# Linear attention and SwiGLU on one core: which engine makes the third part of a hidden chunk

## The chip, the cores and the metric

The kernel runs on one core of a Trainium2 chip. The metric is the device time of one execution in microseconds (us). The core has TensorE (PE, matrix products into PSUM), VectorE (DVE), ScalarE (ACT), GpSimd (POOL) and SyncE (SP); SP, POOL and ACT also issue DMA transfers, each from a queue of its own that works in order. A row `PEld` is the loading of weights into TensorE, which runs beside its products.

## The reference

```python
# attention: q, k, v are (4, 4, 1088, 32); S1, S2 are (8, 32)
def phi(x):
    a = np.einsum('rd,bhsd->bhsr', S1, x)
    b = np.einsum('rd,bhsd->bhsr', S2, x)
    return np.einsum('bhsi,bhsj->bhsij', a, b).reshape(*x.shape[:-1], 64)
q_p, k_p = (phi(q), phi(k))
kv = np.einsum('bhsf,bhsd->bhfd', k_p, v)
z = np.sum(k_p, axis=2)
num = np.einsum('bhsf,bhfd->bhsd', q_p, kv)
den = np.einsum('bhsf,bhf->bhs', q_p, z)[..., None] + 1e-06
x = (num / den).transpose(0, 2, 1, 3).reshape(4352, 128)
# feed-forward: w_gate, w_val are (128, 1536); w_out is (1536, 128)
g = x @ w_gate
silu = g * (1.0 / (1.0 + np.exp(-g)))
out = silu * (x @ w_val) @ w_out
```

All of it is float32.

## The kernel before

The tokens are cut into ten blocks: 0 to 2 are the first batch (384, 320 and 384 tokens), 3 to 8 have 480 tokens each and 9 (`LAST`) has 384. The inner dimension of 1536 is cut into 12 chunks of 128. A *unit* is one block with one chunk j: the gate and value products, a SiLU on ScalarE, and the hidden chunk h = silu * value on VectorE. Later a *down* product multiplies h by its piece of `w_out` and adds it to the block's sum in PSUM. The first 90 us or so hold the attention of the first batch and the units of blocks 0 to 2; the attention of the other batches is strewn between later units.

**The loop this is about** runs over 84 units, y = 0 to 83, twelve for each of blocks 3 to 9 (`line`); block 6 is y = 36 to 47 (from about 172 us), block 7 is 48 to 59, block 8 is 60 to 71 and block 9 is 72 to 83 (from about 248 us). In each pass the program text issues, in this order: the first two matmuls of unit y+1 with ScalarE's scaling of their PSUM pair (`start_unit`, L983 and L986); then `finish_unit` of unit y, which begins with the work on the list `before[y]`, goes on with four matmuls (L995, L996), the SiLU (L998) and VectorE's product (L1003), frees the PSUM pair, and ends with the work on the list `behind[y]`; then up to two stores from the list `going`; then the down products that keep some six chunks waiting (`todo`). Three PSUM pairs serve the units in turn, so the matmuls of unit y+3 can start when L1003 of unit y has read its pair. Every engine works through its own instructions in this order.

**Products in parts.** A matmul of full float32 shows as two records of about 0.4 us each at 480 columns. A chunk on the list `DOWN` goes by three cheaper matmuls instead, on rounded parts. `cut_hidden(y, i, j)` makes the parts of h: the high part h1 is -CUT/BETA times h, rounded; h0 = BETA * h1 + h is what is left; hd = h1 + h0. `down` then multiplies hd (L1063), h1 (L1065) and h0 (L1066) with parts of the weights. The first goes to one bank of PSUM and the other two to another bank, which `copy_out` (ScalarE, L1088) moves to SBUF and `put_together` (VectorE, L1098) adds, after which `store` transposes the sum (L1124) and sends it out (L1134).

- h1 of a chunk of unit y is made in unit y+1: on VectorE, last on the list `before` (L953), for even j outside block 5; on ScalarE, on the list `behind` (L955), for the others.
- hd, for every block but the last: SP copies h1 to hd's place by DMA in unit y+1 (L957); in unit y+2 VectorE makes h0 (L960), and POOL issues a DMA that adds h0 to what lies there (L966). In the last block a VectorE addition makes hd (L964).
- `DOWN` holds seven chunks of block 5, chunks 1 to 10 of blocks 6, 7 and 8, and chunks 1 to 7 of the last block (its first 256 columns; the rest goes through `straight` at the end).

Parts of h live in eight sets of buffers used in turn. Two steps a block prepare the next block's tokens (`cut_tokens`: L865 on ScalarE, L868 on POOL, L873 on VectorE). A finished block gives four stores, or eight where it crosses from one batch into the next.

Of the kernel before, what the change touches and what calls it, by code (L numbers as in the profile page):

```python
# [13 lines left out]
ALU = mybir.AluOpType  # L14
# [5 lines left out]
def kernel(  # L20
# [28 lines left out]
    nc = tc.nc  # L49
# [24 lines left out]
    LAST = len(blocks) - 1  # L74
# [110 lines left out]
    def load_next():  # L185
# [36 lines left out]
        out=ident[:], in_=ident[:], pattern=[[-1, P]], base=0, channel_multiplier=1,  # L222
# [594 lines left out]
    def whole(ap):  # L817
        return ap.bitcast(FP32)
# [67 lines left out]
    line = list(range(HEAD, len(blocks)))  # L886
    FINE = range(1, NCH - 1)
    DOWN = [(line[2], j) for j in (2, 4, 5, 6, 8, 9, 10)]
    DOWN += [(i, j) for i in line[3:6] for j in FINE]
    DOWN += [(LAST, j) for j in range(1, 8)]  # L890
    down_parts = {}
    h_parts = {}
    h_sets = []
    before, behind = {}, {}

    def add_to(where, y, f):
        where.setdefault(y, []).append(f)
# [38 lines left out]
    def cut_hidden(y, i, j):  # L936

        if not h_sets:
            x = []
            for tag in ("kld", "qld", "vld", "kT", "qT"):  # L940
                t = const.tile([P, 2, WB], F32R, tag=tag, name="h" + tag, bufs=1)
                x += [t[:, k, :] for k in range(2)]
            for tag, n in (("late", 8), ("wg", 3), ("wv", 3)):
                t = const.tile([P, n, WB], F32R, tag=tag, name="h" + tag, bufs=1)
                x += [t[:, k, :] for k in range(n)]
            h_sets.extend(x[k : k + 3] for k in range(0, len(x), 3))
        n = SPLIT if i == LAST else blocks[i][1]
        h_sets.append(h_sets.pop(0))
        h1, h0, hd = h_parts[i, j] = [x[:, 0:n] for x in h_sets[-1]]
        h = hidden[i, j][:, 0:n]  # L950
        small = -CUT / BETA
        if j % 2 == 0 and i != line[2]:
            add_to(before, y + 1, lambda: nc.vector.tensor_scalar(h1, h, small, None, op0=ALU.mult))  # L953
        else:
            add_to(behind, y + 1, lambda: nc.scalar.activation(h1, h, AF.Copy, scale=small))  # L955
        if i != LAST:
            add_to(behind, y + 1, lambda: nc.sync.dma_start(out=whole(hd), in_=whole(h1)))  # L957

        def rest():
            nc.vector.scalar_tensor_tensor(  # L960
                out=h0, in0=whole(h1), scalar=BETA, in1=h, op0=ALU.mult, op1=ALU.add
            )
            if i == LAST:
                nc.vector.tensor_tensor(out=hd, in0=whole(h1), in1=whole(h0), op=ALU.add)  # L964
            else:
                nc.gpsimd.dma_start(out=hd, in_=h0, accum_op=ALU.add)  # L966

        add_to(before, y + 2, rest)


# [6 lines left out]
    def start_unit(i, j):  # L977

        n = blocks[i][1]
        xd = x_parts[i][2][:, 0:n]  # L980
        ps = sums_of[i, j] = pair((i, j))[:, :, 0:n]
        for k, w in enumerate((wg, wv)):
            nc.tensor.matmul(  # L983
                ps[:, k], w_parts[id(w), j // 3][2][:, j % 3, :], xd, start=True, stop=True
            )
        nc.scalar.activation(ps, ps, AF.Copy, scale=-1.0 / WHOLE)  # L986

    def finish_unit(i, j, y=None):
        n = blocks[i][1]
        x1, x0, _ = (x[:, 0:n] for x in x_parts[i])  # L990
        ps = sums_of.pop((i, j))
        now(before, y)
        for k, w in enumerate((wg, wv)):
            w1, wb = (w_parts[id(w), j // 3][t][:, j % 3, :] for t in range(2))
            nc.tensor.matmul(ps[:, k], w1, x1, start=False, stop=False, skip_group_check=True)  # L995
            nc.tensor.matmul(ps[:, k], wb, x0, start=False, stop=True, skip_group_check=True)  # L996
        sg = fpool.tile([P, WB], FP32, tag="sg", name="sg", bufs=5)[:, 0:n]
        nc.scalar.activation(sg, ps[:, 0], AF.Silu, scale=WHOLE)  # L998
        slot_of[i, j] = slots.pop(0)
        hj = slot_of[i, j]  # L1000
        hidden[i, j] = hj
        todo.append((i, j))
        nc.vector.scalar_tensor_tensor(  # L1003
            out=hj[:, 0:n], in0=ps[:, 1], scalar=WHOLE, in1=sg, op0=ALU.mult, op1=ALU.mult
        )
        let_go((i, j))
        now(behind, y)
        if (i, j) in DOWN:
            cut_hidden(y, i, j)
# [38 lines left out]
    def down(y=None):  # L1048

        i, j = todo.pop(0)  # L1050
        n = SPLIT if i == LAST else blocks[i][1]
        first = i not in acc
        if first:
            acc[i] = bank("g2" if i == 1 or i in line[2::2] else "acc")
        made[i] = made.get(i, 0) + 1
        mine = [c for c in range(NCH) if (i, c) in DOWN]
        if mine and j == mine[0]:
            acc[i, "p"] = bank("acc" if i in line[2::2] else "g2")
        sides = dict(start=first, stop=(made[i] == NCH))
        if j in mine:  # L1060
            w1, wb, wd = [down_parts[x][:, FINE.index(j), :] for x in ("w1", "wb", "wd")]
            h1, h0, hd = h_parts.pop((i, j))
            nc.tensor.matmul(acc[i][:, 0:n], wd, hd, **sides)  # L1063
            p = acc[i, "p"][:, 0:n]
            nc.tensor.matmul(p, w1, h1, start=(j == mine[0]), stop=False)  # L1065
            nc.tensor.matmul(p, wb, h0, start=False, stop=(j == mine[-1]))  # L1066
            if j == mine[-1]:
                copy_out(y, i, n)
        else:
            nc.tensor.matmul(acc[i][:, 0:n], wo[:, j, :], hidden[i, j][:, 0:n], **sides)  # L1070
        if i != LAST:
            hidden.pop((i, j))
            slots.append(slot_of[i, j])
        if made[i] == NCH:
            if mine:
                put_together(y, i, n)
            elif i == HEAD - 1:

                add_to(behind, 1, lambda: store(i, n))
            else:  # L1080
                store(i, n)
# [36 lines left out]
    going = []  # L1118
# [42 lines left out]
    for h in range(H):  # L1161
# [13 lines left out]
        out=s12[:],  # L1175
# [73 lines left out]
    def parts_of(n):  # L1249

        for _ in range(n):
            if ahead[0] not in ("pe", "end"):
                ahead[0] = next(att, "end")

    def group():
        while ahead[0] != "pe":
            ahead[0] = next(att)
        ahead[0] = next(att, "end")
# [143 lines left out]
    for y in range(END):  # L1402
        if y in GROUPS:
            group()
        at = [(line[x // NCH], x % NCH) for x in (y, y + 1) if x < END]
        if y in WIDE:
            finish_unit(*at[0], y)
        if y + 1 < END:
            start_unit(*at[1])
        if y not in WIDE:  # L1410
            finish_unit(*at[0], y)
        for send in going[:2]:
            send()
        del going[:2]
        for _ in range(2):

            if len(todo) > min(6 + (todo[0] == (line[1], 0)), END - y + 1):
                down(y)
        parts_of(y < EASY or y % 2 == 0)
        for gen in token_steps.get(y, ()):  # L1420
            next(gen, None)
        if y in range(20, 30):
            next(down_steps, None)
# [43 lines left out]
```

## Time and profile before

| | |
|---|---|
| three runs | 280.11, 279.72, 280.16 us; median 280.11 |
| profiled execution | 280.31 us, of which the span from first to last instruction is 278.6 |
| PE busy | 269.8 us (97% of the span), 2195 instructions |
| DVE busy | 203.0 us (73%), 388 |
| ACT busy | 192.4 us (69%), 342 |
| POOL busy | 91.0 us (33%), 114 |
| DMA | 32.51 MB; 28.9% of 16 engines' span on SP's and ACT's queue, 19.0% on POOL's |
| transfers of parts | each 240 KB; 37 copies issued by SP (medians by buffer 2.3 to 4.2 us from issue to landing) and 37 accumulations by POOL (3.2 to 4.5) |

Every row of a timeline has start, length, engine, line, operation, what is written and read, shapes, and in brackets the idle time just before with what ended it. Lengths of neighbouring matmuls, and of neighbouring VectorE operations, overlap, so the distance between starts is what one of them costs. Buffers appear under the names of the tiles whose space they reuse (`hlate`, `hwv`, `hqld` and so on are all parts of h).

### The profile page before, as it was taken

To read this page: it belongs to the slowest core of one execution; us is meant where nothing else is said; L and a number is where in the kernel's file an instruction comes from. 1 tells how busy PE (TensorE), PEld (TensorE's weight loads), DVE (VectorE), ACT (ScalarE), POOL (GpSimd) and SP (SyncE) were. 2 spreads that over 40 slices of the span, in tenths; PEclk is the share of its full clock that TensorE was granted. 3 is DMA by queue.
4 is the path that set the end of the run, shared out by engine and by line. 5 is a ranking of instruction groups with operands and counts; after the bars stand their busy time and mean duration, and the time that the engine had idled before them with its cause. 6 is when DMAs were issued, how large, how long until landed. Compare 5 with 4: busy or idle time off the path is not lost.

```text
span 278.6 us, 5961 instructions
## 1 busy us (share of the span) xinstructions
PE 269.8 (97%) x2195; PEld 200.6 (72%) x2195; DVE 203.0 (73%) x388; ACT 192.4 (69%) x342; POOL 91.0 (33%) x114
## 2 busy tenths in 40 slices
PE   8899999999999999999999999999999999998994
PEld 7645566667885787777677678768877878886894
DVE  3997988899798764897637688559668758873771
ACT  3468566463684877677489889778779869875870
POOL 3314322169150720530055231342343343423000
PEclk9999999999999999999999999999999999999999
DMA  6583195222240043000200169867988997998121
GB/s 193 165 229 93 39 275 176 82 80 87 36 100 11 1 119 90 1 0 3 35 17 1 38 167 186 176 161 179 225 183 206 217 213 174 217 226 181 22 37 28
DMA packets 36797, 32.51 MB, mean 117 GB/s; under 512 B 21024, under 2 KB 34848, under 8 KB 36768
## 3 DMA queue, kind: packets, MB, share of 16 engines
q1 hardware_dynamic: 30784, 22.93, 28.9%
q0 software_dynamic: 5328, 9.10, 19.0%
q8 instruction: 17, 0.28, 0.4%
q10 hardware_dynamic: 656, 0.10, 0.2%
q14 instruction: 12, 0.10, 0.1%
HBM read 11.41 MB, written 2.23 MB: 49 GB/s over the span
## 4 chain that ended last, share of the span: by engine, by line
PE 82%; DMA 10%; DVE 4%; ACT 2%; issue 1%; SPq 0%; POOLq 0%
PE PS L1070 19%; PE PS L983 12%; PE PS L995 12%; PE PS L1019 12%; PE PS L996 11%; DMA hwv<-hwv 5%; DMA hlate<-hlate 2%; PE PS L1063 2%; PE PS L1065 2%; PE PS L1066 2%; PE PS L354 2%; PE PS L342 2%; PE PS L776 2%; PE PS L388 2%; DMA kld<-in_k_dram 2%
## 5 line engine op out<-in xcount | busy, mean ns | idle before, releaser
L986 ACT ACTIVATE PS<-PS 128x960 f32<-128x960 f32 (+1 forms) x90 | 83.2, 925 | 35.0 <-PE PS L983 34.2
L1003 DVE SCALAR_TENSOR_TENSOR hbuf<-PS,sg 128x480 f32<-128x480 f32 (+1 forms) x87 | 55.5, 638 | 51.0 <-ACT sg L998 49.4
L1070 PE MATMUL PS<-hbuf,wo 128*128 128x480 f32 (+3 forms) x126 | 52.6, 514 | 0.0
L998 ACT ACTIVATE sg<-PS 128x480 f32<-128x480 f32 (+1 forms) x90 | 49.6, 551 | 1.6 <-PE PS L996 1.3
L983 PE MATMUL PS<-xd,graw 128*128 128x480 f32 (+1 forms) x69 | 37.1, 537 | 0.0
L983 PE MATMUL PS<-xd,wd 128*128 128x480 f32 (+1 forms) x90 | 33.5, 372 | 0.0
L996 PE MATMUL PS<-x,wb 128*128 128x480 f32 (+1 forms) x90 | 33.5, 372 | 0.0
L995 PE MATMUL PS<-x,w 128*128 128x480 f32 (+1 forms) x90 | 33.4, 371 | 0.0
L1070 PEld LDWEIGHTS PS<-hbuf,wo 128*128 128x128 f32 x126 | 23.6, 189 | 6.1 <-issue 0.4
L996 PE MATMUL PS<-x,graw 128*128 128x480 f32 (+1 forms) x69 | 25.5, 370 | 0.0
L1019 PE MATMUL PS<-xT,wg 128*128 128x384 f32 (+1 forms) x60 | 23.5, 473 | 0.1
L983 PEld LDWEIGHTS PS<-xd,wd 128*128 128x128 f32 x90 | 17.0, 189 | 9.1 <-issue 5.1
L1019 PE MATMUL PS<-xT,wv 128*128 128x384 f32 (+1 forms) x60 | 23.1, 468 | 0.3 <-DVE wv L286 0.3
L1023 ACT ACTIVATE sg<-PS 128x384 f32<-128x384 f32 (+1 forms) x24 | 11.2, 467 | 13.2 <-PE PS L1019 12.4
L966 POOL DMA_DIRECT2D hlate<-hlate x14 | 12.2, 895 | 24.0 <-DMA hlate<-hlate 6.9
L995 PEld LDWEIGHTS PS<-x,w 128*128 128x128 f32 x90 | 16.9, 187 | 2.2
L996 PEld LDWEIGHTS PS<-x,wb 128*128 128x128 f32 x90 | 16.9, 188 | 2.1
L983 PEld LDWEIGHTS PS<-xd,graw 128*128 128x128 f32 x69 | 13.0, 188 | 7.5 <-ACT PS L986 4.3
L995 PE MATMUL PS<-x,graw 128*128 128x480 f32 (+1 forms) x48 | 18.0, 376 | 0.0
L1019 PEld LDWEIGHTS PS<-xT,wv 128*128 128x128 f32 x60 | 11.2, 190 | 7.3 <-DVE hbuf L1034 0.8
L1019 PEld LDWEIGHTS PS<-xT,wg 128*128 128x128 f32 x60 | 10.9, 190 | 7.7 <-issue 1.1
L995 PE MATMUL PS<-x,gphq 128*128 128x480 f32 (+1 forms) x42 | 16.0, 381 | 0.1
(224 smaller groups left out, 525.3 us busy)
## 6 DMA issues: line engine op xcount, KB each, us to landing
hlate<-hlate POOLq DMA_DIRECT2D x14, 240.0 KB, 3.6
kld<-in_k_dram SPq DMA_DIRECT2D x4, 544.0 KB, 4.3
hlate<-hlate SPq DMA_DIRECT2D x9, 240.0 KB, 3.1
vld<-in_v_dram SPq DMA_DIRECT2D x12, 144.0 KB, 4.8
qld<-in_q_dram SPq DMA_DIRECT2D x3, 544.0 KB, 4.8
raw<-in_moe_w_out_dram SPq DMA_DIRECT2D x4, 384.0 KB, 4.7
hqld<-hkld SPq DMA_DIRECT2D x5, 240.0 KB, 4.2
hqld<-hkld POOLq DMA_DIRECT2D x5, 240.0 KB, 3.5
```

The lines of the kernel that those rows point to most:

```text
L342: nc.tensor.matmul(ps[32 * a : 32 * a + 32, 96 * (c - c0) : 96 * (c - c0) + 96], qT[:, 4 * c + a, :], s123[:, a : a + H, :, :].rearrange(" ...
L354: nc.tensor.matmul(ps[32 * a : 32 * a + 64, 64 * (c - c0) : 64 * (c - c0) + 64], kT[:, c, a : a + 2, :].rearrange("p a t -> p (a t)"), s12 ...
L966: nc.gpsimd.dma_start(out=hd, in_=h0, accum_op=ALU.add)
L983: nc.tensor.matmul(ps[:, k], w_parts[id(w), j // 3][2][:, j % 3, :], xd, start=True, stop=True)
L986: nc.scalar.activation(ps, ps, AF.Copy, scale=-1.0 / WHOLE)
L995: nc.tensor.matmul(ps[:, k], w1, x1, start=False, stop=False, skip_group_check=True)
L996: nc.tensor.matmul(ps[:, k], wb, x0, start=False, stop=True, skip_group_check=True)
L998: nc.scalar.activation(sg, ps[:, 0], AF.Silu, scale=WHOLE)
L1003: nc.vector.scalar_tensor_tensor(out=hj[:, 0:n], in0=ps[:, 1], scalar=WHOLE, in1=sg, op0=ALU.mult, op1=ALU.mult)
L1019: nc.tensor.matmul(o[:, 0:n], w[:, j, :], xT[:, t0 : t0 + n], start=True, stop=True)
L1023: nc.scalar.activation(sg[:, 0:n], g[:, 0:n], AF.Silu)
L1070: nc.tensor.matmul(acc[i][:, 0:n], wo[:, j, :], hidden[i, j][:, 0:n], **sides)
```

## The change

For blocks 6, 7 and 8 the DMA way of making hd stays for odd j alone. For even j VectorE makes hd by an addition (L964 of the kernel before) right after h0, and neither SP nor POOL issues a transfer. Block 5 keeps DMA for all its seven chunks, the last block keeps VectorE for all. Where h1 is made on VectorE it is put at the head of the list `before` instead of its end. The last block's chunk 8 joins `DOWN`. Of the waiting stores one is sent in each unit instead of two.

```diff
-    DOWN += [(LAST, j) for j in range(1, 8)]
+    DOWN += [(LAST, j) for j in range(1, 9)]
...
         small = -CUT / BETA
-        if j % 2 == 0 and i != line[2]:
-            add_to(before, y + 1, lambda: nc.vector.tensor_scalar(h1, h, small, None, op0=ALU.mult))
-        else:
+        carried = i == line[2] or i != LAST and j % 2
+        if carried or j % 2:
             add_to(behind, y + 1, lambda: nc.scalar.activation(h1, h, AF.Copy, scale=small))
-        if i != LAST:
+        if carried:
             add_to(behind, y + 1, lambda: nc.sync.dma_start(out=whole(hd), in_=whole(h1)))
+        if not carried and j % 2 == 0:
+            high = lambda: nc.vector.tensor_scalar(h1, h, small, None, op0=ALU.mult)
+            before.setdefault(y + 1, []).insert(0, high)
 
         def rest():
             nc.vector.scalar_tensor_tensor(
                 out=h0, in0=whole(h1), scalar=BETA, in1=h, op0=ALU.mult, op1=ALU.add
             )
-            if i == LAST:
+            if carried:
+                nc.gpsimd.dma_start(out=hd, in_=h0, accum_op=ALU.add)
+            else:
                 nc.vector.tensor_tensor(out=hd, in0=whole(h1), in1=whole(h0), op=ALU.add)
-            else:
-                nc.gpsimd.dma_start(out=hd, in_=h0, accum_op=ALU.add)
...
-        for send in going[:2]:
-            send()
-        del going[:2]
+        if going:
+            going.pop(0)()
```

## The prediction

> **What bounds the kernel now.** I read the busy strip of the page first, then the chain of waits, then the timeline of each engine at the places where the chain leaves TensorE.
>
> ```profile
> PE   8899999999999999999999999999999999998994
> DVE  3997988899798764897637688559668758873771
> ACT  3468566463684877677489889778779869875870
> PEclk9999999999999999999999999999999999999999
> DMA  6583195222240043000200169867988997998121
> ```
>
> TensorE (PE) is filled from end to end at full clock; no other engine is. The DMA engines are idle until slice 23 (about 160 us) and then 80 to 90% busy up to 258 us: that is the stretch in which hidden chunks go through DMA to become hd. So removed matmul time or removed PE waits are worth their length; work on other engines costs only where PE comes to wait for it.
>
> The chain in order of time shows where PE does wait (start, length, what):
>
> ```profile
> 197.93 0.51 ACT PS L986
> 198.44 3.86 DMA hwv<-hwv
> 202.36 0.49 issue
> 202.85 4.38 DMA hwv<-hwv
> 207.28 0.48 PE PS L1063
> ...
> 246.12 3.55 DMA hqld<-hkld
> 249.71 0.48 PE PS L1063
> ...
> 251.49 3.65 DMA hlate<-hlate
> 255.69 3.23 DMA hlate<-hlate
> 258.97 0.48 PE PS L1063
> ```
>
> One part's two transfers in a row, a copy on SP's queue (L957) and an accumulating one on POOL's (L966), end after PE wants the matmul with hd (L1063). The PE timeline gives the size, for instance here:
>
> ```profile
> 253.65 0.34 PE L996 MATMUL PS<-x,wb 128*128 128x384 f32 x1
> 254.61 0.49 PE L1063 MATMUL PS<-hqT,dparts 128*128 128x480 f32 x1 [0.62 <-DMA hqT<-hkT]
> 254.94 0.38 PE L1065 MATMUL PS<-hkT,dparts 128*128 128x480 f32 x1
> ```
>
> Matmuls overlap, so the measure is start to start: 0.175 us after a 384-column one and 0.217 after 480. Here it is 0.96 and then 0.33, so 0.785 + 0.11 = 0.89 lost. Counted so, all stalls before an L1063 are 0.94 (at 206.22), 0.06 (209.34), 0.58 (227.11), 0.35 (249.28), 0.59 (251.35), 0.89 (253.65), 0.61 (256.24) and 0.33 (258.56): **4.35 us**. The down matmul of unit y-6 stands at the end of unit y, so these are chunks 9 and 10 of block 6 (units 51, 52), chunk 7 of block 7 (unit 61), and chunks 6 to 10 of block 8 (units 72 to 76). A check on the last five: L983 starts at 248.40 and 259.72, 11.32 us for five units; a unit with nothing late is 6 x 0.173 + 3 x 0.217 = 1.69, five are 8.45, so 2.87 lost against 2.77 listed.
>
> **The change, part by part.**
>
> (1) Even chunks of blocks 6, 7, 8 (numbered from 0) lose both transfers: 15 copies and 15 accumulations of 240 KB. Even stalls go with them: 0.06 + 0.35 + 0.89 + 0.33 = 1.63 us.
>
> (2) Odd chunks keep both transfers but lose their neighbours. The need: the down matmul is wanted at 206.43 for block 6's chunk 9, whose copy is issued at 198.44, so 8.0 us. Quiet transfers of this size in the table of DMA issues take 2.3 (hlate<-hqT) and 3.2 (hvld<-hvld); the pause between them was 0.5. That is 6.0 us, 2.0 early. With the table's medians for crowded ones (3.1 and 3.6) it is 7.2, still 0.8 early. The tail is tighter: units there last 1.69 instead of 1.95. SP's timeline shows why block 8 suffers most: two stores (L1134, 1.5 to 1.9 us a pair) stand ahead of each copy, and chunk 9's copy left at 249.31 though ACT had made its h1 by 247.11.
>
> With one store per unit, at most some 0.95 stands ahead, so it leaves near 247.6; 6.0 later is 253.6, 7.2 later 254.8. It is wanted at 256.42 less the 1.83 of earlier stalls gone, 254.6. So 1.0 early or 0.2 late. The odd stalls, 0.94 + 0.58 + 0.59 + 0.61 = 2.72, go to between 0 and 0.2; from the other side, if load did not matter at all, they would stay at 2.72. I take 0, by the quiet rows, since half the traffic goes.
>
> The Trainium skill ("DMA: Bandwidth & Descriptors", section on the anatomy of one DMA) has a fixed 2.0 us plus bytes over 436 GB/s, 2.6 us for 240 KB, mostly fixed: taken alone it says that less load buys little. The trace's same-sized transfers range from 2.2 to 5.3 us, so here load is what counts; the page's 2.6 + 0.5 + 2.6 would also be in time.
>
> (3) VectorE gains 15 subtractions hd (L964) of 480 columns. The trace has L964 at 256 columns only, 0.425 us; the 480-column add with one operand in PSUM (L1098) is 0.65:
>
> ```profile
> 190.04 0.65 DVE L873 SCALAR_TENSOR_TENSOR xd<-x,xT 128x480 fp32r<-128x480 f32 x1
> 190.61 0.65 DVE L960 SCALAR_TENSOR_TENSOR hlate<-hqT,hbuf 128x480 fp32r<-128x480 f32 x1
> 191.18 0.67 DVE L1124 STREAM_TRANSPOSE o<-sum 128x480 f32<-128x480 f32 x1
> 191.77 0.37 DVE L953 TENSOR_SCALAR hlate<-hbuf 128x480 fp32r<-128x480 f32 x1
> 192.06 0.65 DVE L1003 SCALAR_TENSOR_TENSOR hbuf<-PS,sg 128x480 f32<-128x480 f32 x1
> ```
>
> Back to back they start 0.57 apart (0.29 to 0.33 for L953). So hd costs 0.57, 8.6 us in all, at most 0.65, 9.8 us. Two units last 2 x 1.95 = 3.90; VectorE works 2 x (0.58 + 0.57) + 0.33 = 2.63 of them now and 3.20 after, 82%. What it must not do is finish L1003 late: in unit y it frees the PSUM pair that the first matmuls of unit y+3 need, with 1.1 to 1.2 us of slack in a plain unit (197.44 + 0.66 against the L983 at 199.24). I added 0.57 to each unit from 42 to 72 that has an even rest, against the SiLU that L1003 waits for. Plain units absorb it. The worst is unit 43 (the rows above): already full, after unit 42 that gained hd and an L1098; L1003 would start 0.75 us after its SiLU, with 0.4 us of slack left. With 0.65 for each operation and no overlap, units 43 to 46 and 67 to 72 run out of slack and PE loses about 0.8. So 0 to 0.8; I take 0.1, near the overlapped starts.
>
> (4) The even high part moves to the head of its unit. It follows the L1003 that makes its input on the same engine, so it waits for nothing. Behind it stand the rest of the unit before, an odd chunk's accumulation on POOL, and L1003; each moves 0.33 later, against the 2.0 and 0.8 us of (2). In units 51 and 63 its old place met POOL's subtraction:
>
> ```profile
> 206.30 1.44 POOL L868 TENSOR_TENSOR x<-xT,x 128x480 fp32r<-128x480 f32 x1
> 206.40 1.61 DVE L953 TENSOR_SCALAR hkT<-hbuf 128x480 fp32r<-128x480 f32 x1
> ```
>
> 1.61 (1.22 in unit 63) instead of 0.40; at the head it would start near 205.9 and be through. That spares VectorE up to 1.2 + 0.8 us, or nothing if POOL, with fewer transfers to issue, starts sooner. Both units have slack, so 0 on PE either way.
>
> The skill speaks against more VectorE work here ("SBUF — State Buffer", section on the two separate sides): an operation with two SBUF inputs, as hd is, and a GpSimd one that reads SBUF exclude each other for their whole length. L960, also with two SBUF inputs, ran 205.84 to 206.49 across that POOL start unstretched. By the rule one POOL subtraction a block could hold hd for 1.44, up to 0.4 past the slack each time, 1.2 us more; by the row nothing.
>
> (5) Stores one per unit: the same number of issues on SP, worked into (2). Block 8's four go in units 79 to 82, long before the last stores at 275.35. 0, hidden by the tail of matmuls; without that cover an SP issue of 0.5.
>
> (6) Chunk 8 of the last block: the fp32 pair of 256 columns (2 x 0.215 = 0.43) becomes three of 0.117 (0.35): 0.08 less. VectorE gets 0.25 + 0.42 + 0.42 more in units 81 and 82, where it idled 1.19 before the L1003 at 269.74. Were that cover gone, the late thing would be this chunk's L1063, by those 1.1 at most. The sum's copy (L1088) moves one unit later, behind the last SiLU; it is needed only at 273.24. 0.
>
> **Sum.** 4.35 + 0.08 - 0.1 = 4.3 off the profiled execution, 280.31 us (span 278.6 and 1.7 around it): 276.0. It stood 0.2 above the median of 280.11, so 275.8. Bounds: 280.11 - 4.43 = 275.7 at best, with 0.4 for noise 275.3; at worst within this case 275.8 + 0.2 + 0.7 = 276.7.
>
> **Rivals.**
>
> Odd transfers stay late. For it: they are still issued in the same units, and a quiet pair needs 6.0 of about 7 us in the tail. Against it: the 2.0 us to spare at unit 51. All 2.72 staying gives 275.8 + 2.7 = 278.5; half of it 277.2.
>
> VectorE becomes the bound, and the kernel is slower. Place: blocks 6 to 8, the pairs of units. It decides once 3.20 exceeds 3.90, so when hd takes over 1.27 us. Price: if each hd were stretched as L953 was beside POOL (1.2 more, 1.77), a pair takes 4.40, 15 x 0.50 = 7.5 us lost, less 4.4 gained: 283.2. For it: that one row, and unit 43 being full already. Against it: L960 keeps 0.65 in all its groups, and POOL gets fewer issues.
>
> No change that shows: under 0.2%, 0.56 us, is all a measurement here can tell. The waits go, but hd at about 1.55 us loses what they gave: 15 x 0.28 = 4.2; 280.
>
> **How the numbers follow.** Forecast 0.64, odd transfers late 0.20, no change 0.05, VectorE bound 0.11. Faster 0.84, same 0.05, slower 0.11. Range 275.3 to 278.6: the forecast's own (275.3 to 276.7) and the second case up to all odd stalls staying; what is left out is 0.16.
>
> **What would show it.** Right: no L1063 that waits for a DMA from 200 to 260 us; copies near 2.3 and accumulations near 3.2 us; DMA digits of 4 to 6 there; L964 of 480 columns near 0.65 with starts 0.57 apart; L1003 after its SiLU within 0.1 us in most units and 0.8 in unit 43; L953 never above 0.5. Wrong: an L983 of units 45 to 48 waiting for L1003; L1063 of odd chunks still late; L964 above 1.2.

## The result and the profile after

Four runs gave 276.66 us (276.21 to 277.50) against 280.13 (279.72 to 280.78) before: a ratio of 0.988, 95% interval 0.985 to 0.991. On another chip, beside other experiments, the changed kernel gave 276.74 against 280.56, 0.987 (0.985 to 0.988). The profiled execution took 276.21 us with a span of 274.5, so 4.1 less than the profiled one before.

The strip of the page, in the same 40 slices:

```profile
PE   6999999999999999999999999999999999999994
DVE  3997988989788774887655677668958986996981
DMA  6673196121231043000110048853464472565021
```

The DMA digits from 199 to 254 us (slices 29 to 36, counted from 0) fell from 7 to 9 down to 2 to 7, VectorE's rose to 9 in places, PE's have no dip left. The chain of waits followed from 196 to 262 us, by line, holds nothing but matmuls; before, 23 us of that stretch (35% of 66) were DMA:

```profile
by line: PE PS L998 22.0%; PE PS L997 21.9%; PE PS L985 21.5%; PE PS L1065 9.5%; PE PS L1068 9.4%; PE PS L1067 9.4%; PE PS L1072 6.8%
```

(The new lines: the matmul with hd is L1065, the unit's first matmuls L985, the SiLU L1000, its product L1005, the high part L958, h0 L962, hd L968, the copy L956.) Here is the PE timeline of unit 73, where the kernel before lost 0.59 us on an odd chunk:

```profile
249.30 0.34 PE L997 MATMUL PS<-x,w 128*128 128x384 f32 x1
249.47 0.34 PE L998 MATMUL PS<-x,wb 128*128 128x384 f32 x1
249.65 0.38 PE L1065 MATMUL PS<-hvld,dparts 128*128 128x480 f32 x1
249.87 0.38 PE L1067 MATMUL PS<-hqld,dparts 128*128 128x480 f32 x1
```

The starts are 0.17, 0.18 and 0.22 apart: nothing waits. All eight listed stalls are gone. The start of each unit's first matmul, compared between the two traces, lies 0.11 us later up to unit 36 and 4.28 us earlier at unit 83, and the steps between fall where the stalls were: 0.93 after unit 51, 0.57 after 61, 2.77 over units 72 to 76.

### The profile page after: what moved, and what is told of

Read it like the earlier page. It is cut to its first block, busy times and chain, and to the rows that moved or that the text cites. A ratio compares the mean times of both kernels' runs of the same rounds, so it can differ in the third digit from the quotient of the medians.

```text
span 274.5 us, 5887 instructions
## 1 busy us (share of the span) xinstructions
PE 267.0 (97%) x2196; PEld 200.7 (73%) x2196; DVE 212.5 (77%) x406; ACT 192.3 (70%) x342; POOL 78.3 (29%) x99
## 4 chain that ended last, share of the span: by engine, by line
PE 92%; DVE 3%; DMA 2%; ACT 1%; issue 0%; SPq 0%
PE PS L1072 19%; PE PS L997 14%; PE PS L985 14%; PE PS L998 14%; PE PS L1021 12%; PE PS L1065 3%; PE PS L1067 3%; PE PS L1068 3%; PE PS L354 2%; PE PS L342 2%; PE PS L776 2%; PE PS L388 2%; DMA kld<-in_k_dram 2%; PE PS L1110 1%; PE PS L497 1%; PE PS L445 1%
## 5 line engine op out<-in xcount | busy, mean ns | idle before, releaser
L1005 DVE SCALAR_TENSOR_TENSOR hbuf<-PS,sg 128x480 f32<-128x480 f32 (+1 forms) x87 | 55.2, 634 | 35.9 <-ACT sg L1000 34.1
L1000 ACT ACTIVATE sg<-PS 128x480 f32<-128x480 f32 (+1 forms) x90 | 49.6, 551 | 2.2 <-PE PS L998 1.9
L985 PE MATMUL PS<-xd,graw 128*128 128x480 f32 (+1 forms) x69 | 37.0, 537 | 0.0
L985 PE MATMUL PS<-xd,wd 128*128 128x480 f32 (+1 forms) x90 | 33.5, 372 | 0.0
L985 PEld LDWEIGHTS PS<-xd,wd 128*128 128x128 f32 x90 | 17.0, 189 | 9.1 <-issue 4.7
L985 PEld LDWEIGHTS PS<-xd,graw 128*128 128x128 f32 x69 | 13.0, 188 | 7.5 <-ACT PS L988 4.3
L868 POOL TENSOR_TENSOR x<-xT,x 128x480 fp32r<-128x480 f32 (+1 forms) x6 | 7.8, 1308 | 35.1 <-ACT x L865 35.1
L966 POOL DMA_DIRECT2D hlate<-hlate x10 | 8.6, 862 | 30.8 <-DVE hwg L962 12.7
```

Source lines behind the costliest of these rows:

```text
L985: nc.tensor.matmul(ps[:, k], w_parts[id(w), j // 3][2][:, j % 3, :], xd, start=True, stop=True)
L1005: nc.vector.scalar_tensor_tensor(out=hj[:, 0:n], in0=ps[:, 1], scalar=WHOLE, in1=sg, op0=ALU.mult, op1=ALU.mult)
```

## The experiments

Stalls are counted as in the prediction, start to start beyond the usual distance, before the matmul with hd. All runs ask the same question from different sides: where did 4.35 us of waiting come from, and what else could have taken or returned it?

### The difference alone

```diff
-    DOWN += [(LAST, j) for j in range(1, 9)]
+    DOWN += [(LAST, j) for j in range(1, 8)]
...
-            before.setdefault(y + 1, []).insert(0, high)
+            add_to(before, y + 1, high)
...
-        if going:
-            going.pop(0)()
+        for send in going[:2]:
+            send()
+        del going[:2]
```

> Of the change only the move of the 15 even differences of blocks 6 to 8 to VectorE; high parts at the end of their list, two stores a unit, last block's chunk 8 in full float32. Waits theory (the eight stalls before hd's matmul, 4.35 us, were the whole gain): 280.1 - 4.35 + 0 to 0.4, so 275.8 to 276.6 profiled, no stall of an even chunk; with two stores ahead of each copy on SP, the odd chunk 9 of block 8 may stay 0 to 0.6 late. Rival, stores (SP's queue, not VectorE, brought the gain): 278 or more, since the pairs of stores stay.

276.49 us (four runs, 276.40 to 277.61) against 281.0 for the kernel before on that chip; ratio 0.984 (0.977 to 0.991). One stall of 0.10 us is left, in unit 73 (block 8's chunk 7; the expectation named chunk 9). So moving the fifteen differences is the change; the other three parts are at most tenths of a us.

### The stores alone

```diff
-        for send in going[:2]:
-            send()
-        del going[:2]
+        if going:
+            going.pop(0)()
```

> The kernel before with only the stores spread, one per unit. Waits theory: all 74 transfers of parts remain, DMA stays 80 to 95% busy from 200 to 256 us, so most stalls stay; copies of block 8 leave SP up to 2 us earlier, worth 0.3 to 1.0 of the 2.8 lost there: 279 to 280. Rival, stores: the stalls of block 8 go (2.8 us) and those of units 51 and 61 shrink: 276.5 to 277.5.

On the kernel before. 280.56 against 281.0, ratio 0.997 (0.993 to 1.000); span 277.5, 1.1 less than the profile before. Stalls in that execution: 0.91 in unit 51, 1.21 in units 60 to 62, 1.34 in units 73 to 76, in all 3.45 against 4.35. Spreading the stores halves the loss of block 8 and adds a little elsewhere. (The profiled execution, 279.17 us, is the fastest of the ten, so other executions may have lost more than these 3.45.) The rival that makes SP's queue the main cause falls.

### The load kept, with nobody waiting for it

```diff
+            if i != LAST:
+                t = (0, 480, 1088, 1568)[j // 2 % 4]
+                aside = xT[:, t : t + n]
+                add_to(behind, y + 1, lambda: nc.sync.dma_start(out=aside, in_=whole(h1)))
...
                 nc.vector.tensor_tensor(out=hd, in0=whole(h1), in1=whole(h0), op=ALU.add)
+                if i != LAST:
+                    nc.gpsimd.dma_start(out=aside, in_=whole(h0), accum_op=ALU.add)
```

> The changed kernel, with the 15 copies and 15 accumulations of the even chunks put back, into dead places of the token tile, where no instruction waits for them; VectorE still makes the even hd. Load theory (odd chunks were late because the DMA engines and POOL's queue were full): odd stalls come back, 1.0 to 2.7 us, so 277.2 to 279 profiled, copies back to 3 to 4 us. Rival, need alone (the odd chunks come in time whatever else is moved, thanks to the stores): within 0.4 of the changed kernel, 276.2 to 276.6.

280.57 us against 281.0, ratio 0.998 (0.995 to 1.001): the whole gain is gone, more than was expected. No even chunk can be late any more (its hd comes from VectorE), and yet the odd ones lose 4.63 us: 1.28 in unit 51, 1.27 in 61, 0.21 in 71, 1.58 in 73, 0.29 in 75. Its chain of waits, in order of time, before the first of them:

```profile
198.52 3.44 DMA hwv<-hwv
202.03 0.49 issue
202.52 5.64 DMA hwv<-hwv
208.21 0.49 PE PS L1071
```

The copy left SP at 198.52, almost the 198.44 of the kernel before, and the accumulation needed 5.64 us (3.68 in the changed kernel), while idle accumulations were in flight beside it. In the PE timeline that is the wait in brackets:

```profile
206.82 0.37 PE L1004 MATMUL PS<-x,wb 128*128 128x480 f32 x1
208.21 0.49 PE L1071 MATMUL PS<-hwv,dparts 128*128 128x480 f32 x1 [1.02 <-DMA hwv<-hwv]
```

Nothing stood before this chunk in POOL's queue: its accumulation was issued 0.56 us after the copy had landed, the usual pause. The same holds for the largest stall, in unit 73 (0.57 us). There the copy took 4.87 us against 2.56 in the changed kernel and the accumulation 4.16 against 3.15. So the transfers themselves were longer; they did not merely start later.

### Half of that load

Only the accumulations, then only the copies, of the edit above.

> The changed kernel with only the 15 accumulations of the even chunks put back, into dead places, no copies. If POOL's queue and the accumulating transfers (4 to 6 us each when two are in flight) are what made odd chunks late: stalls before hd's matmul of 1.5 to 4 us, 277.7 to 280.5. If the copies on SP's queue did it: under 0.5 us of stalls, 276.2 to 276.7.

276.99 us, one run; stalls of 0.32 (unit 59), 0.11 (73) and 0.34 (75), together 0.77.

> The changed kernel with only the 15 copies of the even chunks put back, into dead places, no accumulations. If the accumulations made odd chunks late: under 0.5 us of stalls, 276.2 to 276.7. If the copies did: 1.5 to 4 us, 277.7 to 280.5.

275.85 us, one run; 0.19 in unit 73. Both expectations looked for one guilty half, and neither half brings the 4.6 us. The accumulations do more (hwv's take 4.9 us in the middle, against 3.7 in the changed kernel), but only both together bring the whole effect, as when a shared resource fills up. From 200 to 256 us:

| kernel | DMA busy | stalls before hd's matmul |
|---|---|---|
| changed | 0.51 | 0 |
| with copies | 0.64 | 0.19 |
| with accumulations | 0.83 | 0.77 |
| with both | 0.92 | 4.63 |
| before | 0.92 | 4.35 |

The shares are the last but one number of these rows (here the changed kernel, then the one with both):

```profile
core 0: us, PE busy (x) PEld busy (x) DVE busy (x) ACT busy (x) POOL busy (x), PEclk, DMA share, GB/s
200.00:256.00 56.00, 56.00 (x259) 47.87 (x258) 46.35 (x83) 47.38 (x75) 12.22 (x13) 1.00 0.51 110
200.00:256.00 56.00, 52.66 (x236) 43.41 (x235) 43.93 (x75) 43.52 (x67) 22.03 (x25) 1.00 0.92 204
```

Each row of the table is one profiled execution. The first two cannot be told apart: variants with no added load lose 0 to 0.34 us in unit 73 (below). Which part of the DMA path fills up, the engines or what feeds them, these runs do not separate.

### All differences of blocks 6 to 8 on VectorE

```diff
-        carried = i == line[2] or i != LAST and j % 2
+        carried = i == line[2]
```

> The changed kernel with the odd differences of blocks 6 to 8 on VectorE too: 15 more subtractions, no transfer of parts in these blocks. Overlapped-start theory (0.57 each, a pair of units 3.77 of 3.90): VectorE is full, the units with join, transpose and token difference overrun their slack and PE waits 1 to 4 us in all: 277 to 280. Rival, full length (0.65 each, a pair 4.3 of 3.90): 18 pairs lose 0.4 each, 7 us: 283. Rival, VectorE never binds: 276.2.

281.88 us, ratio to the kernel before 1.003 (1.000 to 1.006), so 5.4 us slower than the difference alone (276.49), timed beside it, though DMA is 6% busy from 200 to 256 us. VectorE is busy 51.8 of those 56 us, and the first matmuls of units wait for L1005 (7.0 us of weight loads by the table of waits). One pair of units on VectorE:

```profile
198.43 0.65 DVE L1005 SCALAR_TENSOR_TENSOR hbuf<-PS,sg 128x480 f32<-128x480 f32 x1
198.99 0.65 DVE L962 SCALAR_TENSOR_TENSOR hwg<-hwg,hbuf 128x480 fp32r<-128x480 f32 x1
199.68 0.66 DVE L968 TENSOR_TENSOR hwg<-hwg 128x480 fp32r<-128x480 f32 x1
200.25 0.65 DVE L1005 SCALAR_TENSOR_TENSOR hbuf<-PS,sg 128x480 f32<-128x480 f32 x1
200.93 0.41 DVE L958 TENSOR_SCALAR hkld<-hbuf 128x480 fp32r<-128x480 f32 x1
201.26 0.65 DVE L962 SCALAR_TENSOR_TENSOR hwv<-hwv,hbuf 128x480 fp32r<-128x480 f32 x1
201.94 0.66 DVE L968 TENSOR_TENSOR hwv<-hwv 128x480 fp32r<-128x480 f32 x1
202.52 0.65 DVE L1005 SCALAR_TENSOR_TENSOR hbuf<-PS,sg 128x480 f32<-128x480 f32 x1
```

From L1005 to the second L1005 after it is 4.09 us; PE would need 3.90. The steps are 0.56, 0.69, 0.57, 0.68, 0.33, 0.68, 0.58. Where an operation reads what the one just before it wrote (L962 to L968, L1005 to L958) the distance is 0.68 to 0.69, elsewhere 0.56 to 0.58, and 0.33 behind the shorter L958. The expectation of 3.77 took no account of that. The 0.2 of a plain pair is not the whole loss: from unit 38 to 75 PE falls 6.0 us behind the changed kernel, about 0.2 in each of six steps and 0.3 to 0.9 in each of seven others. VectorE's other work falls in this stretch too, and three of its operations beside POOL's subtraction took 1.47 to 1.57 us; their shares were not separated. So the five-and-five split is no accident: ten on DMA and ten on VectorE both fill an engine.

### The other three parts undone, one at a time

High part last:

```diff
-            before.setdefault(y + 1, []).insert(0, high)
+            add_to(before, y + 1, high)
```

> The changed kernel with the even high parts at the end of their list again. Own theory: no effect on PE (0 to 0.1 us), L953's form of 480 columns up to 1.2 to 1.6 us once or twice beside POOL's subtraction; but since the operation that reads the result of the one just before it starts 0.68 after it and not 0.57 (seen when all differences were on VectorE), the last place, which has no such neighbour, costs VectorE 0.11 less per even unit, and L1003 is less late after its SiLU in plain units. Rival: the head place is what keeps VectorE in time, and units 43 to 46 or 51 to 52 now hold PE up by 0.3 to 1.5 us.

276.56 us, one run; 0.29 us of stall in unit 73, none in units 43 to 52. L958 meets POOL's subtraction again (1.43 and 1.23 us in units 51 and 63), and L1005 of units 52 to 55 begins about as late after its SiLU as with the head place (0.5 to 1.0 us). In units 65 to 68 it is less late (0.2 to 0.5 against 0.5 to 0.8), as the expectation's own theory had it: at the end of the list L958 stands behind L962, whose result it does not read, and starts 0.57 after it, where behind its own L1005 it starts 0.68 after. So the reading makes the difference, not the operation. Neither place reaches PE.

Two stores a unit:

```diff
-        if going:
-            going.pop(0)()
+        for send in going[:2]:
+            send()
+        del going[:2]
```

> The changed kernel with two stores a unit again. Own theory: stores on SP matter only where a copy of block 8 stands behind a pair: 0 to 0.3 us of stalls, all in units 73 and 75. Rival, stores: 1 us or more of stalls.

276.41 us, one run; 0.25 us of stall, in unit 73.

Chunk 8 of the last block in full float32:

```diff
-    DOWN += [(LAST, j) for j in range(1, 9)]
+    DOWN += [(LAST, j) for j in range(1, 8)]
```

> The changed kernel without chunk 8 of the last block among the parts. Own theory: PE from the first matmul of unit 83 to the last product of the tail is 0.08 us longer, nothing else. Rival: VectorE's three added operations or the later copy of the sum cost the changed kernel something there, and the tail is shorter without them by 0.1 to 0.5.

276.71 us, one run. From the first matmul of unit 83 to the start of the last product of the tail: 6.75 us, as before the change; with chunk 8 in parts 6.67. So 0.08. A stall of 0.34 in unit 73 appears here as well, which this edit cannot cause: block 8's chunk 7 is 0 to 0.34 late in the variants that leave its way alone. Its accumulation landed at 249.92 us here and at 247.96 in the changed kernel's own profile, 1.7 before its matmul, so its transfers vary by some 2 us between executions.

### The changed kernel again

> The changed kernel unaltered, on another chip, timed beside the others. If its first four times (276.2 to 277.5) only scatter: median 276.2 to 277.0 and a trace with no stall before hd's matmul. If some executions have odd chunks late: a trace at 276.8 or more with 0.3 to 1 us of such stalls.

276.74 us, four runs of 276.41 to 276.94. The profiled one (276.78) has no stall after unit 41 but one in block 5:

```profile
173.65 0.38 PE L998 MATMUL PS<-x,wb 128*128 128x480 f32 x1
174.35 0.48 PE L1065 MATMUL PS<-hlate,dparts 128*128 128x480 f32 x1 [0.32 <-DMA hlate<-hlate]
```

0.59 us, in unit 36, on block 5's chunk 6, which both kernels make by DMA while DMA is nearly full (its digits before 200 us are as high as 8). In the first profiled execution the same matmul followed without a gap. That is as much as the 0.57 us between these two profiled executions, and so one cause of the scatter; whether it makes all of it was not tried. The profiles of the load kept and of all differences on VectorE show the same stall (0.51 and 0.61).

### Two more chunks of block 5 in parts

By DMA like their neighbours:

```diff
-    DOWN = [(line[2], j) for j in (2, 4, 5, 6, 8, 9, 10)]
+    DOWN = [(line[2], j) for j in range(2, 11)]
```

> The changed kernel with chunks 3 and 7 of block 5 in parts too (by DMA as its other seven), a try at a faster version. Each spares PE 0.81 - 0.65 = 0.16 us: 0.32 less, 275.9 profiled, if no stall comes. Rival: DMA in block 5 (80 to 100% busy from 160 to 180 us) gets two more pairs and its chunks come late, 0.5 to 2 us of stalls: 276.5 to 278.

277.10 us, six runs of 276.06 to 277.65. The 0.3 us are saved, and 0.7 lost on stalls of 0.43 and 0.27 in units 36 and 37 (chunks 6 and 7; the expectation below says 35 and 36): the DMA engines' busy share from 160 to 180 us is 1.00, against 0.81 in the changed kernel. Then the same two by VectorE:

```diff
-    DOWN = [(line[2], j) for j in (2, 4, 5, 6, 8, 9, 10)]
+    DOWN = [(line[2], j) for j in range(2, 11)]
...
-        carried = i == line[2] or i != LAST and j % 2
+        carried = j not in (3, 7) if i == line[2] else i != LAST and j % 2
```

> The changed kernel with chunks 3 and 7 of block 5 in parts too, their hd made by VectorE. By DMA they brought 0.8 us of stalls in units 35 and 36. Own theory: 2 x 0.16 = 0.32 us less PE work and no stall, VectorE 0.68 later at most in two units with 1.1 of slack: 0.3 faster than the changed kernel. Rival: VectorE is full of attention work there (units 31 to 36) and takes back 0.3 or more.

276.05 us, four runs of 275.91 to 277.03, against 276.74 for the changed kernel, timed beside it; as ratios to the kernel before 0.985 (0.983 to 0.987) and 0.987 (0.985 to 0.988). The intervals overlap, so it is the best median measured and not shown to be faster. In its trace the starts of units 36 and 40 have gained 0.15 and 0.16, as expected; the profiled run, the slowest of the four, lost 0.7 to chunk 6's late transfer and 0.2 in unit 73.

## Why the prediction was right

It said 275.8 us (275.3 to 278.6), faster with 0.84; it was 276.66. By its own steps:

- **The stalls, 4.35.** Right in kind and size: PE's units moved by 4.28 + 0.11 = 4.39 between unit 0 and 83. The difference alone and the load kept show it from both sides. One reading beside it was wrong: the DMA engines are not idle until slice 23, as the prediction's own strip shows (digits up to 9 in the first twelve slices); no term rests on that.
- **(1) Even stalls, 1.63.** Gone, with their transfers.
- **(2) Odd chunks in time, 0 taken of 0 to 2.72, because half the traffic goes.** Right, and load was the reason: with the traffic put back they lost 4.63, beyond the upper bound, which had assumed that they would be no later than before. The tail was rightly called tight, though it is chunk 7, not 9, that sits on the edge. The medians for that stretch fell to 2.2 to 3.2 for copies, but stayed at 3.2 to 3.7 for accumulations; "near 2.3 and near 3.2" was a little low. The Trainium skill's mostly fixed cost ("DMA: Bandwidth & Descriptors", section on the anatomy of one DMA) does not describe this stretch: by it I estimate 2.6 us, and the same accumulation took 3.68 us with half the traffic and 5.64 with all of it. The page gives its fit for transfers that GpSimd issues; the prediction used it for SP's copies as well, which the page does not say.
- **(3) VectorE, 0.57 for each hd and 0 to 0.8 on PE.** PE lost nothing, but the price was too small. hd reads h0, so it starts 0.67 to 0.69 after it, and the head place puts L958 0.68 after the L1005 whose result it reads. A plain pair takes 3.40 of 3.90 (from the L1005 at 194.34 to the second one after it at 197.74), not 3.20. The kernel before could have shown it: in its last block the L964 of 256 columns starts 0.45 us after the L960 whose result it reads, and that L960 lasts 0.42; the prediction took the length of L964 from there but not this distance. Unit 43 in the changed kernel:

```profile
190.50 0.65 DVE L873 SCALAR_TENSOR_TENSOR xd<-x,xT 128x480 fp32r<-128x480 f32 x1
191.06 0.40 DVE L958 TENSOR_SCALAR hlate<-hbuf 128x480 fp32r<-128x480 f32 x1
191.38 0.65 DVE L962 SCALAR_TENSOR_TENSOR hlate<-hqT,hbuf 128x480 fp32r<-128x480 f32 x1
191.95 0.67 DVE L1126 STREAM_TRANSPOSE o<-sum 128x480 f32<-128x480 f32 x1
192.55 0.62 DVE L1005 SCALAR_TENSOR_TENSOR hbuf<-PS,sg 128x480 f32<-128x480 f32 x1
```

L1005 starts 0.91 after the end of its SiLU (191.64), where 0.75 was said; in units 52 to 56 and 64 to 68 it is mostly 0.4 to 0.8 late, where "within 0.1 us in most units" was said. The slack of 1.1 covered it.

- **(4) The head place, 0.** Right for PE. L958 of 480 columns stays at 0.40 to 0.41 everywhere. But the meeting with POOL moved instead of ending (unit 63):

```profile
229.85 0.41 DVE L958 TENSOR_SCALAR hlate<-hbuf 128x480 fp32r<-128x480 f32 x1
230.11 1.02 POOL L868 TENSOR_TENSOR x<-xT,x 128x384 fp32r<-128x384 f32 x1 [4.55 <-ACT x L865]
230.18 1.47 DVE L962 SCALAR_TENSOR_TENSOR hlate<-hqT,hbuf 128x480 fp32r<-128x480 f32 x1
```

L962, with two SBUF inputs, took 1.47 instead of 0.65, since POOL's operation had started 0.07 before it. The row that I set against the Trainium skill's rule ("SBUF — State Buffer", section on the two separate sides: whichever starts first keeps the port) had L960 starting first, so it could not speak against it. The trace agrees with the rule; one meeting cost VectorE 0.8 and PE nothing.

- **(5) Stores, 0, and (6) chunk 8, 0.08.** 0 to 0.25 in one run, within what chunk 7 varies by anyway, and 0.08.

What the forecast missed lies outside these steps. In the two profiles 4.35 + 0.08 became 4.1 because the stretch before unit 0 was 0.11 longer and the time from VectorE's last copy to the end of the span 3.84 instead of 3.55, although the last transfer landed 2.4 after that copy in both. Several variants have the longer ending and several the shorter; why is open. And the median of the four runs is 0.45 above the profiled execution, where I had set it 0.2 below: the forecast took its own execution for typical, and block 5's chunk 6 shows one reason why it was not.

Of the rivals, the late odd transfers came true only with the load kept. VectorE as the bound came true with ten differences a block instead of five: the place was right, and a plain pair there takes 4.09 of 3.90 us.

## What to carry to other kernels

When a stall ends in a DMA, ask whether the transfer is slow by itself or stands in a crowd: keep the traffic and take away its user, as above. Here the late transfers cost at most 0.34 us in all with the DMA engines 51 to 64% busy, 0.77 at 83% and over 4 at 92%, and moving half of the work to an engine with slack freed the other half too. Count VectorE work by distances between starts, and give an operation that reads its predecessor's result its full length.

## What the runs showed of the hardware that was not expected

- Stalls do not grow in proportion to DMA load: with 0.51, 0.64, 0.83 and 0.92 of the engines busy they were 0, 0.19, 0.77 and 4.63 us, in one profile each.
- Two VectorE operations of 480 float32 columns in a row start 0.57 us apart when the second does not read the first one's result, and 0.67 to 0.69 when it does.
